# Routing attention followed by a hard-swish feed-forward layer: the last gated sums of a block move from VectorE to GpSimd while attention runs, and feed-forward items are handed out a little more slowly

## The chip, the core and the metric

The kernel runs on one core of one Trainium2 chip. A core has five engines with their own instruction queues: TensorE (PE; its weight loads are listed as PEld), VectorE (DVE), ScalarE (ACT), GpSimd (POOL) and SyncE (SP, which only issues transfers here). Each engine works through its queue in order and waits on semaphores for the others. The metric is the time of one execution on the device, in microseconds (us).

## The reference, cut to what matters

```python
B, H, S, D = 4, 8, 768, 64        # attention; 16 cluster centroids for each head
q_assign = argmax(q_n @ c_n.T);  k_assign = argmax(k_n @ c_n.T)     # rows normalised
scores = where(q_assign == k_assign, q @ k.T / 8, -1e9)
x = softmax(scores) @ v           # to 3072 tokens of 512
h = x @ w_in                      # 512 -> 2048
out = (h * clip(h + 3, 0, 6) / 6) @ w_out      # 2048 -> 512
```

All inputs and the output are float32; the weights arrive as eight-byte numbers and are decoded on the chip.

## The kernel before, in words

**Attention.** Two heads form a pair; there are 16 pairs. A pair takes 12 steps, n = 12 g + r with r from 0 to 11: two halves of the queries (`hf`) by six blocks of 128 keys (`j`). A step computes scores of both heads on TensorE (L419), exponentials on ScalarE (`ex`, L434, 128x768), adds `ex` into an accumulator on GpSimd (`key_sums`: L454 for the second key block of a half, L457 for the others) and multiplies by v on TensorE (L467). When a half is complete, `divide` multiplies the accumulator by a matrix of ones on TensorE (`pd`, L488), takes the reciprocal on VectorE (`rcp`, L492) and scales the numerator (L493). All small products of the second half of attention (`pd`, the transposes `pqk` and `po`, and the cluster scores `pcs`, L323) share the one PSUM buffer of the pool `psum_t`, through the helper `scratch`; `pcs` of the next pair can start only when `rcp` has read `pd`.

**Feed-forward.** The 3072 tokens are 12 blocks of 256. A block is 15 items: eight `up` items and seven `down` items. An `up(m, i)` handles two of the 16 blocks of the hidden dimension. From block 1 on it uses seven half-size products in place of eight (`halved`, L648, PSUM tiles `uX` and `uY` of a pool with two buffers) with sums on VectorE (L659, L666), a `lift` on ScalarE (L516) and a `clip` on VectorE (L519) which gives the gated rows `g_sb`. The clip of an `up` is put off: it is held in `ending` and issued by `finish()` in the next `up`, and for i = 7 at the end of that item. The second product needs sums of gated rows too: `gated_sums(i)` (L638), four subtractions or additions of 128x256 for each pair of i, directly after the clip of every odd i. The `down` items multiply (L683): parts 0 and 1 take `a11` (kind 0) and `s2` (kind 5), part 0 for the first four i, part 1 for the last four; parts 2 to 6 take the other five kinds over all i.

For block 1 every `up` also has to make sums of weights for the `up` two further on (`first_sums`, L570, four operations on VectorE); later blocks load these from DRAM. `token_sums` (L589) are four more VectorE operations for each block, in `down` part 4 of the block before.

**The order.** It is written out by hand. In the second half of attention (n >= 96, `DECODED`) four steps form a round. `four_by_four` issues scores and exponentials of two steps, then (r = 2, 6, 10) a burst of feed-forward items, alternated with the preparation of the next pair (`turn` at r = 2, `cluster_scores` first of all and `route` at r = 6, `route_turn` at r = 10). At r = 4 and r = 8 it issues the key sums of the two steps before the burst, then at r = 4 the `divide` of the pair before and the products with v, at r = 8 the products with v and in their middle the `divide` of the half just finished; then the key sums of its own two steps. The number of items in a burst follows from `items_by(n)`, the count of items that should be out by step n. Items that are left when attention is over run one after the other (`for item in fill`).

Of the kernel before, what the change touches and what calls it, by code (L numbers as in the profile page):

```python
# [116 lines left out]
def fast_path(ctx, tc, ok, q, k, v, centroids, moe_w_in, moe_w_out, out):  # L117
# [3 lines left out]
    nc = tc.nc  # L121
# [48 lines left out]
    st = {}  # L170
# [11 lines left out]
    def load(g, *names):  # L182
        if g >= NPAIR:
            return
        b, h = divmod(2 * g, H)
        for name in names:
            if name == "v":
                dst = st["v", g] = vp.tile([P, NCH, 2, D], F32, name="vt")
            elif name == "q":
                st["qk", g] = qkp.tile([P, 2, NCH, 2, D], F32, name="qk")  # L190
            if name != "v":
                dst = st["qk", g][:, "qk".index(name)]
            src = {"q": q, "k": k, "v": v}[name]
            for t in range(2):
                nc.sync.dma_start(dst[:, :, t], src[b, h + t].rearrange("(p j) d -> p j d", p=P))
# [9 lines left out]
    def load_weights(i):  # L205
        if i < len(chunks):
            st["raw", i] = rawp.tile([P, WC, 2], U32, name="raw")
            nc.sync.dma_start(st["raw", i], chunks[i][1])
# [56 lines left out]
    def constants():  # L265
        make_identity(nc, ident)
        for t in range(2):
            nc.vector.tensor_reduce(
                out=parity[:, t : t + 1],
                in_=ident.rearrange("p (h t c) -> p t h c", t=2, c=C)[:, t], axis=AX.XY, op=ALU.max,  # L270
            )
        nc.gpsimd.memset(half_c, 0.5)
        nc.gpsimd.memset(low_c, 1.0 / BOUND)
        nc.gpsimd.memset(ones, 1.0)
        nc.gpsimd.memset(w_low, W_LOW)
        nc.gpsimd.memset(one_hot, 0.0)
        for c in range(C):
            nc.gpsimd.memset(number[:, c : c + 1], float(c))

        warm = psum_t.tile([P, 4, P], F32, name="warm", tag="t")  # L280
        for i in range(14):
            nc.tensor.transpose(out=warm[:, i % 4], in_=ident, identity=ident)

    def centroid_norm():
        cn = unit_rows(nc, startp, cen, D)

        nc.scalar.activation(out=w_totals[:, 0, 0:1], in_=w_low, func=ACT.Exp)

        wide = startp.tile([P, 2, D], F32, name="cenwide")
        for t in range(2):  # L290
            nc.vector.tensor_scalar_mul(out=wide[:, t], in0=cn, scalar1=parity[:, t : t + 1])
        st["wide"] = wide

    def centroid_turn():
        pc = scratch([P, P], "pc")
        nc.tensor.transpose(out=pc, in_=st.pop("wide"), identity=ident)
        nc.vector.tensor_copy(out=cnT, in_=pc)
# [5 lines left out]
    def turn(g, part):  # L303
        if part == 0:
            st["xf", g] = xp.tile([P, NC2, P], F32, name="xf")
        qk, xf = st["qk", g], st["xf", g]
        pt = scratch([P, 4, P], "pqk")
        for i in range(4):
            j = part * 4 + i
            nc.tensor.transpose(out=pt[:, i], in_=qk[:, j // NCH, j % NCH], identity=ident)  # L310
        dst = xf[:, part * 4 : part * 4 + 4]
        nc.scalar.copy(out=dst, in_=pt)
        if part == 2:
            st.pop(("qk", g))
# [4 lines left out]
    def cluster_scores(g):  # L319
        c0, xf = (2 * g) % H * C, st["xf", g]  # L320
        ps = scratch([P, 512], "pcs")[:, 0 : NC2 // 4 * P]
        for a in range(4):
            nc.tensor.matmul(  # L323
                ps[a * 2 * C : (a + 1) * 2 * C], lhsT=cnT[:, c0 : c0 + 2 * C], rhs=xf[:, a::4],
                start=True, stop=True,
            )
        cs = st["cs", g] = rtp.tile([P, NC2 // 4, P], F32, name="cs")
        nc.scalar.copy(out=cs, in_=ps)
# [32 lines left out]
    def route_turn(g, part):  # L361
        if part == 0:
            st["xm", g] = xp.tile([P, NC2, P], BF16, name="xm")
        xm = st["xm", g]
        po = scratch([P, NCH, P], "po", BF16)
        for i in range(NCH):
            nc.tensor.transpose(out=po[:, i], in_=one_hot[:, part * NCH + i], identity=ident_q)
        dst = xm[:, part * NCH : (part + 1) * NCH]
        nc.scalar.activation(out=dst, in_=po, func=ACT.Copy, scale=-FAR if part else 1.0)  # L369
# [40 lines left out]
    def scores_qk(n):  # L410
        g, hf, j = where(n)
        st["ps", n] = psum_s.tile([P, 2, 512], F32, name="ps")
        scores_part(n, st["xf", g], True)
# [111 lines left out]
    HF, HC = NFT // 2, DM // 2  # L525
# [66 lines left out]
    def ffn_items(b):  # L592
# [36 lines left out]
        def gated_sums(i):  # L629
            if i % 2 == 0:  # L630
                return
            a11, a21, a12, a22, s1, s2, s4 = (g_sb[:, k, i - 1 : i + 1] for k in range(7))
            eng = nc.vector if i == HF - 1 else nc.gpsimd
            for out_, in0, in1, op in (
                (s1, a21, a22, ALU.add), (s2, s1, a11, ALU.subtract),
                (a21, a11, a21, ALU.subtract), (s4, a12, s2, ALU.subtract),
            ):
                eng.tensor_tensor(out=out_, in0=in0, in1=in1, op=op)  # L638
# [122 lines left out]
    per_batch = NKT * per_pair  # L761
    total = NPAIR * per_pair
    lag_v, lag_d = 2, 4
    up_first = NFT // 2
    per_ffn = NHC * (NFT // 2 + 7)
# [7 lines left out]
    READY, DECODED = per_batch + 2 * lag_d, 2 * per_batch  # L773
    def items_by(n):

        if n <= DECODED:
            return max(n - READY, 0) * up_first // (DECODED - READY)
        return up_first + (n - DECODED) * (per_ffn + 11) // per_batch

    st["early"] = st["free"] = True  # L780
    fill, checks, unmasked = [], [], []
    st["done"], st["valued"] = 0, DECODED - lag_v

# [5 lines left out]
    def ready(m):  # L789
        if m % per_batch == per_batch - 1:  # L790
            fill.extend(ffn_items(m // per_batch))
# [38 lines left out]
    with tc.manual_schedule():  # L830
        nc.scalar.dma_start(cen, centroids.rearrange("h c d -> (h c) d"))
        load(0, "q", "k")
        constants()
        load(0, "v")
        load_weights(0)
        centroid_norm()
        for part in range(3):
            turn(0, part)
        centroid_turn()
        nc.vector.tensor_copy(out=ident_q, in_=ident)  # L840
        load(1, "q", "k")
        cluster_scores(0)
        scores_qk(0)
        route(0)
        scores_qk(1)
        for part in range(2):
            route_turn(0, part)

        for n in range(0, total + lag_d + 2, 2):
            g, r = divmod(n, per_pair)  # L850
            fours = n >= DECODED
            steps = [i for i in (n, n + 1) if i < total]
            prep = prep_items(g + 1, r, fours)
            if fours:
                four_by_four(n, r, steps)
            else:
                for i in steps:
                    scores(i)
                    exponentials(i)
                    key_sums(i)  # L860
                for i in (n - lag_v, n - lag_v + 1):
                    if i >= 0:
                        attn_v(i)
                m = n - lag_d + 1
                if m >= 0 and m % NCH == NCH - 1:
                    later.append(divide(m))
                    ready(m)
            if prep and r == (6 if fours else 4):
                prep.pop(0)()
            if n == DECODED:  # L870
                st["early"] = False
            if r == 6:
                load(g + 2, "q", "k")
                load(g + 1, "v")
            if not fours or r % 4 == 2 or n >= total:
                want = min(items_by(n + 2) - st["done"], len(fill))
                st["done"] += want
                for i in range(max(len(prep), want)):
                    if i < want:
                        fill.pop(0)()  # L880
                    if i < len(prep):
                        prep[i]()
            for step in decode[: share[r]]:
                step()
            del decode[: share[r]]
            if not fours:
                for op in numbers:
                    op()
                numbers.clear()
                check_all()  # L890
            checks.extend(later)
            later.clear()

        while checks:
            check_all()
            checks.extend(later)
            later.clear()
        for item in fill:
            item()

# [384 lines left out]
```

## Time and profile before

| | before |
|---|---|
| device time, median of 3 | 1040.2 us (1039.38 to 1041.11) |
| profiled span | 1041.0 us |
| TensorE matmul busy | 1005.3 us, 97% |
| VectorE busy | 600.4 us, 58% |
| GpSimd busy | 411.0 us, 39% |
| ScalarE busy | 389.6 us, 37% |
| gated sums on GpSimd (L638) | 144 instructions, 743 ns mean |
| gated sums on VectorE (L638) | 48 instructions, 747 ns mean |
| key sums on GpSimd (L457, L454) | 160 instructions, 1.9 us each |

TensorE is busy in all but 36 us of the span, so a change can shorten the kernel only by taking work from TensorE or by removing some of the times in which it stands still; the list of waits and the timeline show where these are. Second-half attention, with feed-forward items between its steps, runs from about 250 to 841 us of the span; after that the rest of the items follow.

### The profile page before, as it was taken

To read this page: it belongs to the slowest core of one execution; us is meant where nothing else is said; L and a number is where in the kernel's file an instruction comes from. 1 tells how busy PE (TensorE), PEld (TensorE's weight loads), DVE (VectorE), ACT (ScalarE), POOL (GpSimd) and SP (SyncE) were. 2 spreads that over 40 slices of the span, in tenths; PEclk is the share of its full clock that TensorE was granted. 3 is DMA by queue.
4 is the path that set the end of the run, shared out by engine and by line. 5 is a ranking of instruction groups with operands and counts; after the bars stand their busy time and mean duration, and the time that the engine had idled before them with its cause. 6 is when DMAs were issued, how large, how long until landed. Compare 5 with 4: busy or idle time off the path is not lost.

```text
span 1041.0 us, 16706 instructions
## 1 busy us (share of the span) xinstructions
PE 1005.3 (97%) x6560; PEld 742.6 (71%) x6560; DVE 600.4 (58%) x1117; ACT 389.6 (37%) x764; POOL 411.0 (39%) x331
## 2 busy tenths in 40 slices
PE   8999989999999999999997999999999999999997
PEld 4444445546777788776785778787787788989996
DVE  4799976868577355356348236537346273727270
ACT  6888866675233233143232233323323111102010
POOL 3777757666225226227136026316226221303030
PEclk9999999999999999999999999999999999999999
DMA  6455654522222232241232223223032140414120
GB/s 153 120 142 143 162 142 114 142 75 55 56 102 97 54 98 73 54 120 51 54 105 66 54 89 85 58 84 102 8 97 74 44 110 26 143 42 140 50 62 25
DMA packets 107176, 90.34 MB, mean 87 GB/s; under 512 B 78416, under 2 KB 88656, under 8 KB 107088
## 3 DMA queue, kind: packets, MB, share of 16 engines
q1 hardware_dynamic: 106944, 89.15, 31.1%
q8 instruction: 54, 0.88, 0.4%
q14 instruction: 34, 0.28, 0.1%
q10 hardware_dynamic: 144, 0.03, 0.0%
HBM read 73.43 MB, written 15.73 MB: 86 GB/s over the span
## 4 chain that ended last, share of the span: by engine, by line
PE 85%; DVE 5%; ACT 5%; DMA 3%; issue 1%; SPq 1%; ACTq 0%; DVEq 0%
PE Y L683 16%; PE uY L648 14%; PE ps L419 13%; PE X L683 12%; PE uX L648 11%; PE pv L467 10%; PE ph L603 3%; PE pqk L310 2%; PE pd L488 2%; PE pcs L323 1%; ACT ex L434 1%; DVE g_sb L638 1%; DVE g_sb L519 1%; ACT xm L369 1%; DMA raw<-in_moe_w_in_dram 1%
## 5 line engine op out<-in xcount | busy, mean ns | idle before, releaser
L457 POOL TENSOR_TENSOR acc<-acc,ex 128x768 f32<-128x768 f32 x128 | 244.8, 1912 | 207.2 <-ACT ex L434 201.4
L638 POOL TENSOR_TENSOR g_sb<-g_sb 128x256 f32<-128x256 f32 x144 | 104.0, 743 | 310.1 <-DVE g_sb L519 307.3
L434 ACT ACTIVATE ex<-ps 128x768 f32<-128x768 f32 x192 | 148.1, 804 | 85.1 <-PE ps L419 72.8
L516 ACT ACTIVATE sx<-g_sb,half_c 128x512 f32<-128x512 f32 x88 | 63.5, 722 | 286.0 <-DVE g_sb L659 286.0
L419 PE MATMUL ps<-xf 64*128 64x384 f32 x768 | 166.5, 511 | 2.5 <-ACT ex L434 2.5
L467 PE MATMUL pv<-ex,vt 128*64 128x384 f32 x768 | 141.1, 496 | 0.0
L690 DVE TENSOR_TENSOR y<-y,Y 128x256 f32<-128x256 f32 x48 | 20.2, 420 | 152.2 <-PE Y L683 151.4
L492 DVE RECIPROCAL rcp<-pd 128x384 f32<-128x384 f32 x32 | 81.7, 2554 | 42.7 <-PE pd L488 42.5
L467 PEld LDWEIGHTS pv<-ex,vt 128*64 128x64 f32 x768 | 48.7, 136 | 78.2 <-issue 70.0
L419 PEld LDWEIGHTS ps<-xf 64*128 64x128 f32 x768 | 63.5, 187 | 53.6 <-issue 37.7
L648 PE MATMUL uX<-xb,w_in_sb 128*128 128x128 f32 x704 | 93.2, 275 | 0.0
L454 POOL TENSOR_TENSOR acc<-ex 128x768 f32<-128x768 f32 x32 | 60.5, 1892 | 81.4 <-ACT ex L434 81.4
L683 PE MATMUL X<-w_out_sb,g_sb 128*128 128x256 f32 x384 | 91.1, 386 | 0.2 <-DVE sx L659 0.2
L683 PE MATMUL Y<-T,g_sb 128*128 128x256 f32 x384 | 87.2, 380 | 0.0
L683 PE MATMUL Y<-w_out_sb,g_sb 128*128 128x256 f32 x384 | 87.2, 380 | 0.0
L648 PEld LDWEIGHTS uX<-xb,w_in_sb 128*128 128x128 f32 x704 | 85.8, 192 | 0.0
L683 PEld LDWEIGHTS X<-w_out_sb,g_sb 128*128 128x128 f32 x384 | 72.3, 193 | 13.1 <-issue 3.4
L683 PEld LDWEIGHTS Y<-T,g_sb 128*128 128x128 f32 x384 | 72.3, 190 | 11.1 <-issue 1.6
L683 PEld LDWEIGHTS Y<-w_out_sb,g_sb 128*128 128x128 f32 x384 | 72.3, 190 | 11.1 <-issue 1.6
L519 DVE SCALAR_TENSOR_TENSOR g_sb<-sx,g_sb 128x512 f32<-128x512 f32 x88 | 77.1, 879 | 1.2 <-ACT sx L516 1.0
L666 DVE COPY sx<-uX 128x128 f32<-128x128 f32 x88 | 25.6, 291 | 73.7 <-PE uX L648 70.4
L419 PE MATMUL ps<-xm 64*128 64x384 bf16 x384 | 63.1, 323 | 3.1 <-ACT xm L369 2.8
(110 smaller groups left out, 1459.0 us busy)
## 6 DMA issues: line engine op xcount, KB each, us to landing
tx<-td SPq DMA_DIRECT2D x80, 384.0 KB, 3.2
raw<-in_moe_w_in_dram SPq DMA_DIRECT2D x16, 512.0 KB, 3.9
raw<-in_moe_w_out_dram SPq DMA_DIRECT2D x16, 512.0 KB, 3.9
qk<-in_q_dram SPq DMA_DIRECT2D x32, 192.0 KB, 3.8
qk<-in_k_dram SPq DMA_DIRECT2D x32, 192.0 KB, 4.2
vt<-in_v_dram SPq DMA_DIRECT2D x32, 192.0 KB, 4.3
xd<-num SPq DMA_DIRECT2D x32, 192.0 KB, 2.9
xb<-xd SPq DMA_DIRECT2D x12, 512.0 KB, 4.1
```

The source lines that it names most:

```text
L419: nc.tensor.matmul(st["ps", n][:, t, 0:HALF], lhsT=x[r, NCH + j], rhs=x[r, hf * NHC : (hf + 1) * NHC], start=first, stop=not first or by_v ...
L434: nc.scalar.activation(out=ex, in_=sc, func=ACT.Exp, scale=SM_SCALE)
L454: nc.gpsimd.tensor_tensor(out=acc, in0=st["ex", n - 1], in1=ex, op=ALU.add)
L457: nc.gpsimd.tensor_tensor(out=acc, in0=acc, in1=ex, op=ALU.add)
L467: nc.tensor.matmul(pv[t * D : (t + 1) * D], lhsT=vt[:, j, t], rhs=ex[:, t], start=(j == 0), stop=(j == NCH - 1),)
L492: nc.vector.reciprocal(out=rcp, in_=pd)
L516: nc.scalar.activation(out=r, in_=h, func=ACT.Relu, bias=half_c, scale=1.0 / 6.0)
L519: nc.vector.scalar_tensor_tensor(out=g, in0=r, scalar=1.0, in1=h, op0=ALU.min, op1=ALU.mult)
L603: nc.tensor.matmul(ph[:, t * HC : (t + 1) * HC], lhsT=w_in_sb[:, kt, f * P : (f + 1) * P], rhs=st["xb", b, m][:, kt], start=(kt == 0), sto ...
L638: eng.tensor_tensor(out=out_, in0=in0, in1=in1, op=op)
L648: nc.tensor.matmul(dst, lhsT=w[:, kt], rhs=x(kt), start=(kt == 0), stop=(kt == HK - 1))
L683: nc.tensor.matmul(bank[:, half * HC : (half + 1) * HC], lhsT=g_sb[:, kind, i], rhs=w[:, i], start=(first and i == 0), stop=(last and i == ...
```

## The change

Two edits. First, the four sums after the last clip of a block (i = 7) were always on VectorE; now they are on GpSimd, as those of i = 1, 3 and 5 are, as long as attention runs, and on VectorE in the items that run after it. Second, in the second half the number of items due by step n grows by 53/48 a step (45 items of three blocks, and 8) instead of 56/48 (45 and 11).

```diff
@@ gated_sums
-            eng = nc.vector if i == HF - 1 else nc.gpsimd
+            eng = nc.vector if i == HF - 1 and st["last"] else nc.gpsimd
@@ items_by
-        return up_first + (n - DECODED) * (per_ffn + 11) // per_batch
+        return up_first + (n - DECODED) * (per_ffn + 8) // per_batch
 
     st["early"] = st["free"] = True
+    st["last"] = False
@@ after the loop over n
+        st["last"] = True
         for item in fill:
             item()
```

## The prediction

> **What bounds the kernel now.** I read the page first: how busy the engines are, and the chain that ended last.
>
> ```profile
> PE 1005.3 (97%) x6560; PEld 742.6 (71%) x6560; DVE 600.4 (58%) x1117; ACT 389.6 (37%) x764; POOL 411.0 (39%) x331
> PE 85%; DVE 5%; ACT 5%; DMA 3%; issue 1%; SPq 1%; ACTq 0%; DVEq 0%
> ```
>
> TensorE sets the time. Neither edit takes work from it, so all that can be won is among its idle 1041.0 - 1005.3 = 35.7 us, plus the matmuls that run slowly after a pause. The second view is therefore TensorE's own waits, largest first:
>
> ```profile
> PE pcs L323 <- DVE rcp L492: 8.9, 2, 7.1
> PE uX L648 <- DVE sx L659: 6.2, 5, 1.9
> ```
>
> These 15.1 us are all waits for VectorE (the rest is the start, the end, and waits of some us in the first half). Third, the timeline around the longest, with the burst 4u4 to 4u7 (block 4, items `up` 4 to 7) just over at 557.97:
>
> ```profile
> 559.00 8.42 POOL L457 TENSOR_TENSOR acc<-acc,ex 128x768 f32<-128x768 f32 x4
> 559.79 0.87 PE L488 MATMUL pd<-acc,ones 128*64 128x384 f32 x4
> 559.88 1.98 DVE L519 SCALAR_TENSOR_TENSOR g_sb<-sx,g_sb 128x512 f32<-128x512 f32 x1 [0.25 <-ACT sx L516]
> 561.90 7.75 DVE L638 TENSOR_TENSOR g_sb<-g_sb 128x256 f32<-128x256 f32 x4
> ...
> 569.57 2.54 DVE L492 RECIPROCAL rcp<-pd 128x384 f32<-128x384 f32 x1
> ...
> 572.17 1.50 PE L323 MATMUL pcs<-xf,cnT 128*32 128x384 f32 x8 [7.12 <-DVE rcp L492]
> ...
> 573.61 3.64 PE L683 MATMUL X<-w_out_sb,g_sb 128*128 128x256 f32 x8
> ```
>
> `pd` is ready at 560.7, but the reciprocal stands in VectorE's queue behind the clip and the four sums of i = 7. Those should take 0.68 and 4 x 0.42 us; beside the key sums of GpSimd they take 1.98 and 7.75. `pcs` needs the buffer that `rcp` must read. Fourth, the line of the sums shows the two prices:
>
> ```profile
> L638 POOL TENSOR_TENSOR g_sb<-g_sb x144: 722/728/1188, 166.6 to 1009.7; 128x256 f32<-128x256 f32 x144
> L638 DVE TENSOR_TENSOR g_sb<-g_sb x48: 416/424/2048, 253.3 to 1012.7; 128x256 f32<-128x256 f32 x48
> ```
>
> Minimum, median, maximum in ns: 424 alone, up to 2048 beside a key sum. Last, the end of attention, and the granted clock by windows of 8 us (the clock is the column after POOL):
>
> ```profile
> 842.74 0.87 PE L488 MATMUL pd<-acc,ones 128*64 128x384 f32 x4
> 844.75 2.54 DVE L492 RECIPROCAL rcp<-pd 128x384 f32<-128x384 f32 x1
> 848.79 0.71 PE L648 MATMUL uX<-xs,tx 128*128 128x128 f32 x4 [1.86 <-DVE sx L659]
> ```
> ```profile
> 568.00:576.00 8.00, 3.83 (x14) 2.14 (x15) 4.68 (x3) 1.69 (x5) 1.37 (x1) 0.63 0.24 64
> 848.00:856.00 8.00, 7.21 (x49) 7.21 (x50) 5.01 (x16) 1.44 (x2) 2.81 (x4) 0.79 0.31 88
> ```
>
> Here the reciprocal comes between `up` items, delays VectorE's reading of `uX`, and TensorE pauses. After both pauses the clock is low for some us, a cost beyond the wait.
>
> **What the Trainium skill says.** "GPSIMD Engine Reference", section Specifications, says that GpSimd shares its SBUF interfaces with VectorE and contends with VectorE instructions that have two SBUF inputs. The trace agrees: L638 and L519 (two SBUF inputs) stretch from 0.42 and 0.68 to about 2 us beside key sums, while L659, with a PSUM input, stays at 0.29. Section Elementwise of the same page puts a two-input operation at about twice VectorE's time; here it is 728 against 424 ns, 1.7 times. "TensorE: Matmul & The Clock Gate", Part 1, says that an idle window of about 3.4 us brings half the clock until a busy one has passed. The trace agrees after 7.12 us, but shows a low clock after 1.86 us too, and none after the 1.76 us wait at 494.86.
>
> **The change, part by part.**
>
> (a) Which sums move. 12 blocks have four sums each for i = 7. With the new rate, 8 + (198 - 96) x 53 / 48 = 120 items are out when the steps end, exactly blocks 0 to 7; blocks 8 to 11 run after attention and stay on VectorE. So 8 x 4 = 32 instructions go: GpSimd has 176, VectorE 16. VectorE loses 32 x 0.42 = 13.6 us of bare work and more in stretched time; GpSimd gains 32 x 0.73 = 23.3 us on 411. GpSimd sits idle between its groups (L638 alone had 310 us of idle time before it), so its total is no limit.
>
> (b) The new wait on GpSimd. Its queue is in program order: the moved sums come before the key sums of the next two steps. These now wait for the clip of i = 7 and then 4 x 0.73 = 2.9 us. Around 558 this means: VectorE's sums and clips, not contended now, end at 557.97 + about 2.7 = 560.7; sums on GpSimd to 563.6; four key sums of 1.9 to about 571.3 instead of 567.4. Who waits for them? The exponential that needs this `ex` buffer comes six steps later, the `divide` that needs this accumulator at least a burst (some 15 us) later. So nobody, at 4 us late. Who waits for the sums themselves? `down` part 1, for `s2` of i = 6 and 7. From TensorE's end of `up` 7 to the clip is about 2.5 us (482.24 to 484.72 at another block: three additions, lift, clip), plus two GpSimd operations, 1.5: 4.0. TensorE gets there after part 0 (3.5), the first product of part 1 (1.7) and two chunks (0.9): 6.1. One key sum in the way (1.9) just fits, two would cost some 2 us. The three blocks where part 1 follows the `up`s in one burst (1, 3, 6) have the key sums of the step done by then, by about 2 us. I take 0; the upper end is 3 x 2 = 6 us.
>
> (c) The waits removed. Counting `items_by` out gives the bursts. Before, `up` 7 stands at or near the end of the r = 2 burst twice: n = 134 (3u5 3u6 3u7 3d0) and n = 146 (4u4 to 4u7); right after comes r = 4 with `divide`. After, only n = 122 does so (2u4 to 2u7); block 3 ends in n = 138, block 4 in n = 150, both r = 6.
> - n = 146: 7.12 us wait. Slow clock: `pcs` to X takes 1.44 against 0.78 at 494.86, eight X matmuls 3.47 against 1.83; together 2.3. Sum 9.4 us.
> - n = 134: 1.76 us, no slow clock.
> At n = 122 in the new kernel: clip done by start of r = 4 plus 2.7, `pd` done at the same time, `rcp` done at 5.3, `pcs` due at 572.17 - 7.12 - 557.97 = 7.1. Margin 1.8 us, so no wait. Either edit alone might do much of this.
>
> (d) The end of attention. Before, the last `divide` (n = 196) is followed by 8u4 to 8u6, which need VectorE at once. After, it is followed by 7d5 and 7d6, 2 x 3.5 = 7 us of TensorE work that VectorE's 2.54 + 0.56 us hide behind. Removed: 1.86 and the slow clock, in which the next `up` took 4.86 us (848.79 to 853.65) against 3.16 for its neighbours, 1.7: 3.6 us.
>
> (e) Block 1. The waits of 1.59, 0.50 and 1.85 (3.9 us, between 310 and 321) have another cause: in these `up`s VectorE also makes L570, and needs 3.9 us for an item (310.97 to 314.86), 5.25 with GpSimd sums beside it, where TensorE needs 3.12 (3.6 with a `po`). Before, the n = 106 burst was 1u2 to 1u6, after it is 1u1 to 1u5: five such items again. Walking it through: first item free, then TensorE waits about 1.0, 2.5 and 0.8: 4.3, so 0.4 lost. If the 2.5 brings a slow clock, VectorE as the limit hides most of it. Range: 2 won to 3 lost.
>
> (f) The seven items (8u0 to 8u6) that now run after attention cost TensorE 3.16 us each wherever they are, as the tail is without a pause from 856 to 1032: 0.
>
> Sum: -9.4 - 1.8 - 3.6 + 0.4 = -14.4. 1040.2 - 14.4 = 1025.8, I say 1026.
>
> **The rivals.**
> 1. Half of it: a pause of some us comes back elsewhere, since the new bursts have other ends (five `up`s at n = 134, 162 and 174, where a `divide` or `route` needs VectorE beside clips and GpSimd sums), or the first `down`s wait for GpSimd (b). For it: margins of only 1.8 and 2 us. Against: before, bursts of four `up`s without i = 7 (n = 158, 170, 182) gave waits of 0.4 at most. Time: 1026 + 6 = 1032.
> 2. Slower: GpSimd's sums or the new spacing make two waits of the kind of 572. For it: a burst's end decides, and the ends are dealt anew. Against: the worst ingredient, 7.75 us of stretched sums in VectorE's queue, is gone everywhere in attention. Time: 1040.2 - 14.4 + 2 x 9.4 = 1044.6.
> 3. No change: `rcp` was late for another reason, such as the accumulator from GpSimd. Against: `pd` was issued at 559.79 without a wait, and VectorE was busy without a break from 558.95. Time: 1040.
> 4. More: (e) also comes out better and small waits go: 1022.
>
> **How the numbers follow.** The forecast has 0.62, rival 1 0.20, rival 2 0.06, rival 3 0.04, rival 4 0.08. The range takes in (e) at its best and rival 1 with the 6 us of (b) and a few us of slow clock: 1021 to 1036. Faster by over 0.2% (below 1038.1): 0.62 + 0.20 + 0.08 = 0.90. Same 0.03, slower 0.07.
>
> **What would show it.** Right: TensorE's wait of `pcs` for `rcp` gone or below 1 us, L638 on VectorE 16 times at a median and maximum near 424 ns, 176 on GpSimd, no wait of `uX` where attention ends, no window below clock 0.9 after 250 us but for the last, waits of `uX` in block 1 near 4 us, TensorE's busy time lower by some 4 us (fewer slow matmuls). Wrong in (b): waits of TensorE's L683 for GpSimd's L638, or of L434 for L457 longer than 2 us. Wrong in (c): a wait for `rcp` at another burst. The forecast is wrong as a whole if the span falls by less than 4 us.

## The result, and the profile after

| | before | after |
|---|---|---|
| device time, median | 1040.06 us (1039.38 to 1041.11, 4 runs) | 1029.7 us (1026.24 to 1032.62, 4 runs) |
| ratio to before | | 0.9898, 95% interval 0.9866 to 0.9931 |
| profiled span | 1041.0 us | 1024.4 us |
| mean granted TensorE clock of that run | 0.992 | 0.997 |

10.4 us were won where 14.4 were forecast; 1029.7 lies between the forecast (1026) and the first rival (1032). The profiled run after is the fastest of its four and the one with the highest clock, so its span flatters the change: the traces differ by 16.6 us. First the page of the changed kernel, engines and chain:

```profile
PE 997.8 (97%) x6560; PEld 738.4 (72%) x6560; DVE 562.8 (55%) x1085; ACT 390.0 (38%) x764; POOL 433.3 (42%) x363
PE 84%; ACT 4%; DVE 4%; DMA 4%; SPq 2%; issue 1%; POOL 0%; ACTq 0%; DVEq 0%; POOLq 0%
```

TensorE's idle time went from 35.7 to 1024.4 - 997.8 = 26.6 us, so 9.1 of the 16.6 us come from waits and 7.5 from matmuls that ran faster in this run (the prediction had some 4). VectorE lost 37.6 us of busy time for 13.6 us of bare work moved; nearly all of the rest was stretching, of the sums and of the clips before them. Now TensorE's waits:

```profile
PE uX L648 <- DMA tx<-td: 3.8, 2, 2.3
PE ps L419 <- ACT xm L369: 2.8, 5, 1.3
PE ps L419 <- ACT ex L434: 2.6, 8, 0.5
PE uX L648 <- DVE sx L659: 2.2, 3, 1.9
```

The wait of `pcs` for `rcp` (8.9 us before) is no longer in the list, and that of `uX` for VectorE fell from 6.2 to 2.2. At the top stands a wait that had 0.3 us before: the first half-size product of an `up` waits for its weight sums `tx` from DRAM. The line of the gated sums (minimum, median, maximum in ns):

```profile
L638 POOL TENSOR_TENSOR g_sb<-g_sb x176: 723/728/1707, 161.9 to 993.1; 128x256 f32<-128x256 f32 x176
L638 DVE TENSOR_TENSOR g_sb<-g_sb x16: 418/422/426, 846.1 to 996.1; 128x256 f32<-128x256 f32 x16
```

What is left on VectorE runs when there are no key sums, and none of it is stretched. Two bursts still end with `up` 7 in front of a `divide`: n = 122 (the r = 4 `divide` follows) and n = 162 (the r = 8 one). The timeline at n = 122, where the r = 4 scores begin at 403.92:

```profile
405.74 0.87 PE L488 MATMUL pd<-acc,ones 128*64 128x384 f32 x4
405.83 0.69 DVE L519 SCALAR_TENSOR_TENSOR g_sb<-sx,g_sb 128x512 f32<-128x512 f32 x1 [0.25 <-ACT sx L516]
...
406.60 2.91 POOL L638 TENSOR_TENSOR g_sb<-g_sb 128x256 f32<-128x256 f32 x4 [1.60 <-DVE g_sb L519]
406.65 2.56 DVE L492 RECIPROCAL rcp<-pd 128x384 f32<-128x384 f32 x1
...
409.46 7.80 POOL L457 TENSOR_TENSOR acc<-acc,ex 128x768 f32<-128x768 f32 x4
...
410.93 0.85 PE L323 MATMUL pcs<-xf,cnT 128*32 128x384 f32 x8
```

Compare it with 559 to 572 of the kernel before (in the prediction). The clip takes 0.69 in place of 1.98, because GpSimd now stands in front of it, waiting for it, and starts no key sum; the reciprocal follows at once; `pcs` starts 1.7 us after it ends and waits for nothing. The end of attention, where `rcp` made TensorE pause before:

```profile
811.02 2.56 DVE L492 RECIPROCAL rcp<-pd 128x384 f32<-128x384 f32 x1 [1.79 <-PE pd L488]
...
814.46 3.62 PE L683 MATMUL Y<-T,g_sb 128*128 128x256 f32 x16
...
817.91 0.61 PE L648 MATMUL uX<-xs,tx 128*128 128x128 f32 x4
```

The two `down`s of block 7 cover it. Last, the new wait (SPq lines are issues of transfers with the time the issuing took):

```profile
548.89 1.24 SPq L195 DMA_DIRECT2D qk<-in_q_dram  x2
...
550.18 1.33 SPq L195 DMA_DIRECT2D qk<-in_k_dram  x2
...
551.56 2.57 SPq L195 DMA_DIRECT2D vt<-in_v_dram  x2
...
554.23 1.94 SPq L573 DMA_DIRECT2D tx<-td  x3
...
558.57 0.68 PE L648 MATMUL uX<-xs,tx 128*128 128x128 f32 x4 [2.31 <-DMA tx<-td]
```

This is the r = 6 burst of n = 150. Six loads of q, k and v are issued ahead of the burst's items, from 548.89 to 554.13, and the `tx` of an `up` two items on comes behind them, at 554.23. TensorE can use it 4.3 us later, where the median from issue to landing is 3.2 us for `tx`; so both the place in the queue and a slower transfer have a part in the wait of 2.31 us. Before, the r = 6 bursts had at most three `up`s while attention ran; with the new rate four of them (n = 150, 162, 174, 186) have three to five. TensorE waits at the first two. They are the only ones of the four with all six loads in front: at n = 174 no pair is left whose q and k could be loaded, at n = 186 nothing is left to load.

### The profile page after: what moved, and what is told of

Same layout as the page of the kernel before. It is cut to its first block, busy times and chain, and to the rows that moved or that the text cites. A ratio compares the mean times of both kernels' runs of the same rounds, so it can differ in the third digit from the quotient of the medians.

```text
span 1024.4 us, 16727 instructions
## 1 busy us (share of the span) xinstructions
PE 997.8 (97%) x6560; PEld 738.4 (72%) x6560; DVE 562.8 (55%) x1085; ACT 390.0 (38%) x764; POOL 433.3 (42%) x363
## 4 chain that ended last, share of the span: by engine, by line
PE 84%; ACT 4%; DVE 4%; DMA 4%; SPq 2%; issue 1%; POOL 0%; ACTq 0%; DVEq 0%; POOLq 0%
PE Y L683 16%; PE uY L648 14%; PE ps L419 12%; PE X L683 12%; PE uX L648 11%; PE pv L467 9%; PE ph L603 3%; SPq L195 2%; PE pd L488 2%; PE pqk L310 2%; DMA raw<-in_moe_w_in_dram 1%; ACT ex L434 1%; PE pcs L323 1%; DMA tx<-td 1%; DVE wunit L247 1%
## 5 line engine op out<-in xcount | busy, mean ns | idle before, releaser
L457 POOL TENSOR_TENSOR acc<-acc,ex 128x768 f32<-128x768 f32 x128 | 241.3, 1885 | 139.0 <-ACT ex L434 132.6
L638 POOL TENSOR_TENSOR g_sb<-g_sb 128x256 f32<-128x256 f32 x176 | 130.5, 763 | 325.9 <-DVE g_sb L519 322.5
L519 DVE SCALAR_TENSOR_TENSOR g_sb<-sx,g_sb 128x512 f32<-128x512 f32 x88 | 66.9, 764 | 1.0 <-ACT sx L516 0.9
L659 DVE TENSOR_TENSOR g_sb<-uY,sx 128x128 f32<-128x128 f32 (+1 forms) x176 | 65.7, 414 | 0.1
```

The lines of the kernel that those rows point to most:

```text
L457: nc.gpsimd.tensor_tensor(out=acc, in0=acc, in1=ex, op=ALU.add)
L519: nc.vector.scalar_tensor_tensor(out=g, in0=r, scalar=1.0, in1=h, op0=ALU.min, op1=ALU.mult)
L659: nc.vector.tensor_tensor(out=out_, in0=in0, in1=in1, op=ALU.add)
```

## The experiments

All were timed against the kernel before on the same chip, in groups that share its runs. "L639" and the like are the same operations in files that a line or two shifted.

**The changed kernel again.**

> The changed kernel once more, so that the others of this group can be compared with it on one chip. Median of its first four runs 1029.7 us (1026.2 to 1032.6). If the spread comes from where the low-clock stretches fall, the runs again spread over some 5 us, and the span falls by about as much as the mean clock rises (0.001 of mean clock is about 1 us). If it came from the chip of the first runs, they lie within 2 us as those of the kernel before do.

Measured: 1032.64 us (1027.58 to 1034.38, 6 runs), ratio 0.9916 (0.9894 to 0.9939). The spread is there again. Over the ten runs of both groups, the span and mean clock of each run lie near a line (correlation -0.91) with 1.3 us less span for each 0.001 more clock: 1024.4 us at 0.997, 1030.7 at 0.992. So most of the spread goes with the low-clock stretches. Cut into finer windows, the traces show what such a stretch is: 3.4 us at a clock of 0.50 (sometimes two or three times that), which costs 1.7 us. After 250 us and before the last 30, the first profile of the changed kernel has one, at 308.2 us; this one has two, at 312.6 and at 633.5 us, the second behind a wait for `tx`.

**Each edit alone**, against the changed kernel:

```diff
# sums only
-        return up_first + (n - DECODED) * (per_ffn + 8) // per_batch
+        return up_first + (n - DECODED) * (per_ffn + 11) // per_batch
# rate only
-            eng = nc.vector if i == HF - 1 and st["last"] else nc.gpsimd
+            eng = nc.vector if i == HF - 1 else nc.gpsimd
```

> Only the first edit: sums of i = 7 on GpSimd during attention, items at the old rate. My theory (the waits for the reciprocal come from stretched sums in VectorE's queue): the 7.1 and 1.8 us waits of pcs go, with the slow clock behind the first, 9.4 + 1.8 = 11.2 us; the wait where attention ends (1.9 us and slow clock) stays, and there are no waits of uX for tx; so about 1029 us, as fast as the whole change. Rival (the spacing of the items does it, the engine of the sums doesn't matter): 1038 to 1041 us, with pcs waiting for rcp as before.

Measured: 1029.86 us (1028.91 to 1030.73), ratio 0.9908 (0.9893 to 0.9922). The waits of `pcs` are gone, and no `tx` wait appears. The wait at the end of attention stays, as this line of its timeline shows:

```profile
836.45 0.71 PE L648 MATMUL uX<-xs,tx 128*128 128x128 f32 x4 [1.88 <-DVE sx L659]
```

It was followed by no low clock (the next `uX` at 839.68, 3.23 us on). The first edit alone gives as much as both.

> Only the second edit: items at the new rate, all sums of i = 7 on VectorE. My theory: the one burst that still ends with up 7 in front of a divide (n = 122) gives the wait of pcs for rcp of some 7 us with its slow clock, the other two go, the wait at the end of attention goes, the two waits for tx come (4 us): about 1035 to 1039 us. Rival (spacing does it all): 1029 us, no wait of pcs for rcp.

Measured: 1045.14 us (1041.25 to 1049.57), ratio 1.0049 (1.0030 to 1.0068): the second edit alone makes the kernel slower, more than my range had it. Its timeline at n = 122 repeats the picture of before, and after n = 162 there is a second one:

```profile
414.30 7.75 DVE L638 TENSOR_TENSOR g_sb<-g_sb 128x256 f32<-128x256 f32 x4
...
421.97 2.54 DVE L492 RECIPROCAL rcp<-pd 128x384 f32<-128x384 f32 x1
...
424.57 1.50 PE L323 MATMUL pcs<-xf,cnT 128*32 128x384 f32 x8 [7.11 <-DVE rcp L492]
```
```profile
659.02 7.76 DVE L638 TENSOR_TENSOR g_sb<-g_sb 128x256 f32<-128x256 f32 x4
...
666.70 2.54 DVE L492 RECIPROCAL rcp<-pd 128x384 f32<-128x384 f32 x1
...
669.30 0.49 PE L367 MATMUL po<-ident_q,one_hot 128*128 128x128 bf16 x6 [3.70 <-DVE rcp L492]
```

The second I had not counted: the burst n = 162 ends with 5u7 (5u3 to 5u7), so the r = 8 `divide` meets the same clogged queue, and the `po` of the r = 10 burst needs the buffer. Its 3.7 us and the low clock that follows (3.4 us at 0.50, so 1.7 us more) are most of the 6 us by which the measured time is above my range.

**Is it the engine, or what runs beside it?** Rate only, with one copy added that makes GpSimd wait for VectorE's sums:

```diff
+    gate = const.tile([P, 2, 1], F32, name="gate")
...
+            if i == HF - 1 and not st["last"]:
+                nc.gpsimd.tensor_copy(out=gate, in_=s4[:, :, 0:1])
```

> New rate, the sums of i = 7 on VectorE as in the run with the rate alone (1045 us), and one added copy of two columns of s4 on GpSimd after them while attention runs. The copy waits for VectorE's sums and so holds back GpSimd's key sums until they are done. Theory (the loss is the stretching beside key sums, not VectorE's own 4 x 0.42 us): the sums and the clip before them take 0.42 and 0.68 us again, the waits of 7.1 us (pcs) and 3.7 us (po) for rcp fall to below 1 us each, and the time is 1030 to 1034 us. Rival (what counts is that VectorE has the sums in its queue ahead of rcp): half or more of these waits stay, 1038 to 1045 us.

Measured: 1030.57 us (1025.03 to 1031.68), ratio 0.9902 (0.9876 to 0.9928): with the sums still on VectorE, as fast as the change. The line of the sums and the timeline at n = 122:

```profile
L639 DVE TENSOR_TENSOR g_sb<-g_sb x48: 415/422/427, 251.9 to 1000.7; 128x256 f32<-128x256 f32 x48
```
```profile
408.76 1.56 DVE L639 TENSOR_TENSOR g_sb<-g_sb 128x256 f32<-128x256 f32 x4
410.23 2.55 DVE L493 RECIPROCAL rcp<-pd 128x384 f32<-128x384 f32 x1
410.38 0.18 POOL L641 COPY gate<-g_sb 128x2 f32<-128x2 f32 x1 [3.18 <-DVE g_sb L639]
410.51 7.66 POOL L458 TENSOR_TENSOR acc<-acc,ex 128x768 f32<-128x768 f32 x4
...
413.12 0.85 PE L324 MATMUL pcs<-xf,cnT 128*32 128x384 f32 x8
```

The four sums take 1.56 us where rate only took 7.75, though they stand ahead of the reciprocal as before, and `pcs` starts without a wait. The waits of `pcs` and `po` for `rcp` are gone from the list. So the loss was the key sums running at the same time; the first edit works because it puts these behind the clip and the sums in one queue, and a 0.18 us copy does as well.

**How far the sums on GpSimd are from hurting.**

```diff
# all on GpSimd, after attention too
-            eng = nc.vector if i == HF - 1 and st["last"] else nc.gpsimd
+            eng = nc.gpsimd
# s1 and s2 of i = 7 three times over during attention
-                (s1, a21, a22, ALU.add), (s2, s1, a11, ALU.subtract),
+                *[(s1, a21, a22, ALU.add), (s2, s1, a11, ALU.subtract)]
+                * (3 if i == HF - 1 and not st["last"] else 1),
```

> The changed kernel with the sums of i = 7 on GpSimd after attention too (blocks 8 to 11). My theory (down part 1 reaches s2 of i = 6 and 7 about 2 us after GpSimd has it): no wait of L683 for L638, the same time as the changed kernel, 1029 to 1033 us. Rival (s2 from GpSimd comes too late when nothing lies between up 7 and the downs): each of four blocks waits 1 to 3 us, so 1034 to 1044 us.

Measured: 1031.37 us (1029.95 to 1035.93), ratio 0.9923 (0.9899 to 0.9947). No wait of TensorE for L638 is listed; from 830 to 1000 us it waited 0.2 us, for VectorE. The condition `st["last"]` is worth nothing that these runs can tell.

> The changed kernel with s1 and s2 of i = 7 computed three times over on GpSimd while attention runs (the same values; 8 operations in place of 4): s2 comes 2.9 us later, and the key sums behind it too. My theory (margin of s2 about 2 us in the three blocks where part 1 follows in the same burst, more elsewhere; key sums have a burst of slack): at most 3 waits of about 1 us, 0 to 3 us more than the changed kernel, 1030 to 1035 us. Rival (GpSimd is now close to a bound, the moved sums are already paid for in waits): each of 8 blocks 2.9 us longer, some 23 us, about 1053 us.

Measured: 1033.57 us (1031.92 to 1036.05), ratio 0.9947 (0.9924 to 0.9969). Among TensorE's waits is now

```profile
PE X L684 <- POOL g_sb L639: 2.4, 3, 1.0
```

three times, 1.0 us at most: the margin of `s2` is 2.9 - 1.0 = 1.9 us where it is smallest.

**The new wait for tx.**

```diff
-            if r == 6:
+            if r == 6 and not fours:
                 load(g + 2, "q", "k")
                 load(g + 1, "v")
...
+            if r == 6 and fours:            # after the items of the burst
+                load(g + 2, "q", "k")
+                load(g + 1, "v")
```

> The changed kernel, with the loads of q, k and v in the second half issued after the items of the r = 6 burst in place of before them. My theory of the new waits of uX for tx (2.3 and 1.4 us at two r = 6 bursts): the six loads of the pair stand ahead of tx in SyncE's queue and fill the DMA engines; with them behind the burst's own tx loads both waits go, 3 to 4 us less than the changed kernel: about 1026 us. Rival (tx is late because its buffer, three deep, comes free late): no change, 1029 to 1030 us, waits for tx as they are.

Measured: 1028.02 us (1026.82 to 1030.21), ratio 0.9890 (0.9872 to 0.9908), beside 1032.64 for the changed kernel in the same group. TensorE has no wait for `tx` in the list, which begins with

```profile
PE ps L419 <- ACT ex L434: 3.9, 9, 0.7
PE ps L419 <- ACT xm L369: 2.8, 5, 1.3
PE uX L648 <- DVE sx L659: 2.8, 5, 1.9
```

So the `tx` was late because of the loads, and not because its buffer came free late. Whether their place in SyncE's queue or their share of the DMA engines counts for more isn't separated: the edit moves both.

> Late loads with the old rate, sums on GpSimd during attention: the first edit alone with late loads. My theory: in its r = 6 bursts hardly an up stands behind the loads, so they have nothing to give; the wait of uX at the end of attention (1.9 us, sometimes with slow clock) stays: 1029 to 1031 us, as the first edit alone. Rival (late loads help whatever the rate): 1026 us.

Measured: 1029.09 us (1027.58 to 1034.04), ratio 0.9905 (0.9878 to 0.9932): as the first edit alone, as expected where hardly an `up` stands behind the loads; but this interval is 5 us wide.

**A try at block 1**, on top of the late loads:

```diff
-            for out_, in0, in1 in ((t1, b12, b11), (t2, b22, t1), (t4, b21, t2), (b12, b22, b12)):
-                nc.vector.tensor_tensor(out=out_, in0=in0, in1=in1, op=ALU.subtract)
+            for eng, out_, in0, in1 in (
+                (nc.vector, t1, b12, b11), (nc.vector, t2, b22, t1),
+                (nc.gpsimd, t4, b21, t2), (nc.gpsimd, b12, b22, b12),
+            ):
+                eng.tensor_tensor(out=out_, in0=in0, in1=in1, op=ALU.subtract)
```

> The kernel with late loads, and of the four weight sums for each item of block 1 (first_sums) the last two on GpSimd. My theory (in block 1 VectorE is the limit, 3.9 us for an item, with 0.84 us in these two): the waits of uX for sx around 300 us of the span fall from 2 to 3 us to below 1, and the low clock there becomes rarer: 1 to 3 us less than with late loads alone, 1025 to 1027 us. Rival (GpSimd's 1.5 us more stretch VectorE's other two-input operations as much): no change, 1028 us.

Measured: 1025.76 us (1021.74 to 1026.85), ratio 0.9876 (0.9849 to 0.9903). But the wait did not go; in its place stands one of the same length for GpSimd:

```profile
PE uX L651 <- POOL w_in_sb L573: 1.9, 1, 1.9
```

So I ran it and late loads alone once more, side by side.

> The kernel with late loads once more, next to the next one on one chip: about 1028 us (1026 to 1030).

Measured: 1024.73 us (1023.96 to 1025.88), ratio 0.9857 (0.9831 to 0.9884).

> Late loads and split weight sums once more: about 1025.5 us, 1 to 4 us below late loads alone if the split is worth what the first group showed; the same as late loads if that difference came from the low-clock stretches.

Measured: 1025.28 us (1024.11 to 1027.38), ratio 0.9867 (0.9840 to 0.9894). The split gives nothing that can be told; the try failed. No version found is faster than late loads alone, 1.1% and 1.4% under the kernel before in two groups. That they beat the change is likely and not settled: the trace has lost its waits for `tx` (4.9 us in the changed kernel of the same group), and the medians are 1028.02 and 1032.64, but the intervals of the ratios overlap and they met in one group only.

## Why the prediction was right, step by step

**(a)** 176 and 16 instructions, as counted.

**(b)** Right in size. The key sums behind the moved ones ended at 417.3, that is 13.3 us after the start of r = 4, as was worked out; nobody waited for `s2`, and the three-fold sums found the margin at 1.9 us (2 forecast) in three places (three forecast). One sign that I had named against it did appear: an exponential waited 3.2 us for a key sum, where the longest before was 2.0. The moved sums are not its cause: the run with the rate alone, which has them on VectorE, shows 3.2 us too, and the run with the sums alone 2.0. TensorE's waits for exponentials were 2.6 us against 2.5 before; in all the profiles they lie between 2.2 and 4.6 (3.6 with the rate alone), so no cost of the moved sums shows there.

**(c)** Right. The wait of n = 146 and of n = 134 went. `rcp` at n = 122 ended 5.3 us into r = 4, as forecast. The count of bursts looked at r = 2 only and so missed n = 162; with the sums on GpSimd nothing waits there either. "Either edit alone might do much of this" was right for the sums and wrong for the rate: new bursts with `up` 7 at the end (n = 122 and 162) take the place of the old ones, and the rate only moves the collision.

**(d)** The wait went. Its second term, 1.7 us of low clock, was right for the profile it was read from, but isn't a certain cost: with the sums alone the same wait of 1.88 us had no low clock behind it.

**(e)** I forecast waits of 4.3 us; the trace has 0.23 and 1.85, then a window from 304 to 312 us at clock 0.79, where I expected no window under 0.9 outside the ends. Slower matmuls then hid the third, but that is the smaller part. Three other profiles with the new rate have no low clock there (the copy, all sums on GpSimd, late loads again), and their waits are 0.2, 1.9 and 0.5, together 2.6 us. So the walk made the waits too long: where I had 0.4 us lost, the new bursts win 1.3 (3.9 before, and 3.9 with the sums alone).

**(f)** Right: no wait of TensorE is listed from 830 us to the end.

**The term that was missing** is the wait for `tx`. The second edit puts three to five `up`s into r = 6 bursts, where the pair's loads go out first; 3.8 to 5.3 us in the profiles of the change and of the variants with its rate and early loads, 0.3 before. (The one with the copy has 2.7, and at its second such burst a pause of 1.7 us that the list puts down to VectorE's clip.) In some of these runs a stretch of low clock follows, 1.7 us more. I had looked at what the new burst ends do to VectorE's queue, not at what stands in SyncE's. 14.4 less about 4 is the 10.4 measured, but the agreement to a tenth is chance: (e) came out 1.7 us better than forecast, and the runs of one kernel spread over 6 us. Rival 1, "a pause of some us comes back elsewhere", had the kind of loss right; of its places n = 162 is one of the two, but it named VectorE there, and the wait was for a transfer.

The profiles also show what the second edit does. It removes the pause at the end of attention (1.9 us, at times with low clock), shortens those in block 1 by 1.3, and brings the `tx` waits: with the sums on GpSimd, the old rate (0.9908) and the new (0.9916 in the same group) can't be told apart.

## What to carry to other kernels

When two-input VectorE operations stand in front of something TensorE needs, look at what GpSimd runs at that moment: the stretch shows as a mean far above the minimum in the line's own durations (747 against 416 ns here). Moving the work to GpSimd and making GpSimd's long operations wait for it cured it equally well here (ratios 0.9916 and 0.9902); what counted was that the two did not run at the same time. And when work is spread anew over time, follow every queue at the new places, the transfer queue too: a burst that lands behind a group of loads finds its own data late.

## What the runs showed that I had not expected

A pause of 1.85 to 1.9 us on TensorE is followed by a low clock in some runs (848.79 us before, 307.99 us after) and not in others (1.88 us with the sums only; 1.85 us at the same place in block 1 with late loads again), and one of 3.01 us in the run with the rate alone had none. The low stretches of one trace do not start at the end of a pause, but on a grid. Before, they begin at 146.88, 570.14 and 850.04 us, which is 124 and 82 times 3.413 us apart, and the shortest last 3.4 us; the other traces with two or more stretches show the same step, with the grid elsewhere relative to the start of the execution. "TensorE: Matmul & The Clock Gate" of the Trainium skill, Part 1, calls the observed window free-running, which fits: whether a pause brings a low clock would then depend on where on the grid it falls, and that differs from run to run. But a pause of 1.85 us can't leave a whole step of 3.4 us idle, and yet a low clock follows in some runs; how much of a step has to be idle, these runs don't say.

The stretching is nearly one-sided. Beside VectorE's sums, four key sums took 8.42 us before (7.99 with the rate alone) and 7.80 without them, 2 to 8% more, while VectorE's 0.42 us operations took up to 2.05, about the length of one key sum: an operation of VectorE seems to wait for the end of GpSimd's. That it waits in this way is read from the durations, and wasn't tried by itself.
